# wo_B in the buffer of q's weights, M_B's units spread between two products: one change to a gated pair of linear-attention blocks

## The chip, the cores and the metric

The kernel runs on one core of a Trainium2 chip. The metric is device time in microseconds (us) for one execution. The profile is one execution of the same program, taken by the hardware profiler. The engines are called as the profile calls them: PE is TensorE (its weight loads are listed as PEld), DVE is VectorE, ACT is ScalarE, POOL is GpSimd, SP is SyncE. SP and ACT also issue DMAs; in the rows these stand as SPq and ACTq.

## What is computed

```python
def _A_ref(x, wqkv, wo):                      # _B_ref is the same with B's weights
    B, S, D = x.shape                         # 1, 2048, 640
    H = 32; Dh = D // H                       # 20
    q, k, v = ...                             # x @ wqkv, split, by heads
    phi = lambda t: jnp.where(t > 0, t + 1, jnp.exp(t)) + 1e-6
    pq, pk = phi(q), phi(k)
    kv = jnp.einsum("bhsd,bhse->bhde", pk, v)
    z = jnp.einsum("bhsd->bhd", pk)
    num = jnp.einsum("bhqd,bhde->bhqe", pq, kv)
    den = jnp.einsum("bhqd,bhd->bhq", pq, z)[..., None] + 1e-6
    return merge_heads(num / den) @ wo

x = A_x                                       # both blocks read A_x
g = sigmoid((x * gate_w).sum(-1, keepdims=True))
return g * _A_ref(x, A_wqkv, A_wo) + (1 - g) * _B_ref(x, B_wqkv, B_wo)
```

## The kernel before, in words

For each block b (A, then B) the kernel makes pk = phi(x Wk) by row chunks (`k_chunk`), pqT = phi(x Wq) transposed (`q_unit`), G = x^T pk (`g_all`, the row `gs` for its seven half-size products), the block-diagonal part of Wv^T G (`kv_mm` and `kv_mask`, tile KVA), and from that M = KVA wo, a 640x640 matrix (`m_a` for A, `m_b` for B). The gate and the denominators become rows R that scale pqT (`scale`). The output is pqT_A^T M_A + pqT_B^T M_B.

That last sum is a 2x2 block product: rows in two halves of 1024, columns in two halves of 320. It is done in seven products, P1 to P7, over eight pairs of row tiles (class `Pair`; pair i holds row tiles i and i+8). One product of one pair is five matmuls of 128x320 (`prod`, L586 to L592; in the profile all of them are line L590). P1 = pqT_A(lower rows) x M_A(left columns) and P5 = (pqT_A + pqT_B, upper rows) x TM[0], where TM[0] comes from M_A alone. P2, P3, P4, P6 and P7 need M_B, or differences TM[1..3] made from it. So P1 and P5 of the eight pairs, 16 x 5 matmuls, are what the kernel has to do while M_B is made.

M_B is made by six units, `m_b(0)` to `m_b(5)` (L784): two matmuls (L494, KVA rows times wo_B, one for each column half) into two PSUM banks, one copied by ACT and one by DVE (both L791) into a row of pk, then a store to DRAM (`m_store`, L500, queue of SP). After the six, `m_load(1)` (L503, SP) reads all of M_B back in the layout that the products need. The units use four single banks in turn, so unit k+2 writes the banks that unit k's copies empty.

P1 and P5 of one pair share a PSUM bank (`early`): P1 starts it, ACT copies it out (`p1_out`, L623), P5 adds onto it, ACT copies it out again (`p5_out`, L631). The bank then serves pair i+4. P5 of pair i reads upper rows i of pqT_A to which pqT_B has been added in place. That sum is `p_sums(..., (1,))` (L546): POOL makes it for pairs 0 and 1 (the first 256 rows), DVE makes it for pairs 2 and 3, 4 and 5, 6 and 7, in three instructions after the units' copies. DVE then makes the sums for P6 and P3 (also L546) and TM[1..3] (`m_sum`).

The order of everything here is written out by hand: the stages stand under `manual_schedule`, each engine takes its instructions in the order of the code, and the framework adds the semaphores. In the middle stage the order on PE is: P1 of pair 0; `kv_mm`; P1 of pairs 1 and 2; units 0, 1; P1 of pair 3; units 2, 3; P5 of pair 0; units 4, 5; then P5 of 1, P1 of 4 and 5, P5 of 2 and 3, P1 of 6 and 7, P5 of 4 to 7; then P2 (the rows `ow` and `oy`).

Weights go through the pool `wpool`, one buffer for each tag, and a tile of the same tag waits until the earlier one is no longer read. wo_B has the tag `wo`, which before it holds T13, operands of G's products for B. Its six DMAs (`load_wo`, L692 and L694, queue of SP) therefore stand in the code behind the last product that reads T13 (L424). R's second row for B is loaded by the queue of ACT (`r_load`, L543, called in L413).

At the end, the last pair does P7, then pair 6's P3, then its own P4, then its own P3 in two halves of 160 columns; each result is added by DVE (L595) and stored (L609).

Of the kernel before, what the change touches and what calls it, by code (L numbers as in the profile page):

```python
# [8 lines left out]
P = 128  # L9
FP32 = mybir.dt.float32  # L10
BF16 = mybir.dt.bfloat16
# [3 lines left out]
S, D, H = 2048, 640, 32  # L15
Dh = D // H
DT = D // P
# [4 lines left out]
HF = D // 2  # L22
TW = 4
WB = (120, 120, 80)
NW = 6
# [3 lines left out]
SH = S // 2  # L29
# [3 lines left out]
def kernel(  # L33
# [11 lines left out]
    nc = tc.nc  # L45
# [5 lines left out]
    wpool = ctx.enter_context(tc.tile_pool(name="wpool", bufs=1))  # L51
# [18 lines left out]
    xT = persist.tile([P, DT, S], BF16, name="xT")  # L70
    xn = persist.tile([P, ST, D], BF16, name="xn")
    pk = persist.tile([P, ST, D], BF16, name="pk")
    pqT = [persist.tile([P, DT, S], BF16, name=f"pqT{b}") for b in "AB"]
# [3 lines left out]
    M = [persist.tile([P, DT, D], BF16, name=f"M{b}") for b in "AB"]  # L77
    wo_sb = [None, None]
# [23 lines left out]
    TM = [early[:, 0:DT * HF].rearrange("p (c n) -> p c n", c=DT)] + [None] * 3  # L102
# [12 lines left out]
    wq = [None, None]  # L115
# [27 lines left out]
    for r in range(2):  # L143
        nc.gpsimd.memset(maskE[r][:], 1.0)
        for sign, base in ((1, 0), (-1, Dh - 1)):
            nc.gpsimd.affine_select(
                out=maskE[r][:], in_=maskE[r][:], pattern=[[-sign * Dh, WT[0] // Dh], [0, Dh]],
# [4 lines left out]
    for sign, base in ((1, 0), (-1, TW - 1)):  # L152
        nc.gpsimd.affine_select(
            out=headE[:], in_=headE[:], pattern=[[-sign * TW, H]],
# [220 lines left out]
    def g_strassen(b, den):  # L375

        x11, x12 = [xn[:, k:k + hc, 0:ic] for k in (0, hc)]
        x22 = xn[:, hc:ST, ic:2 * ic]
        b11 = pk[:, 0:hc, 0:HF]
        b21, b22 = [pk[:, hc:ST, n * HF:(n + 1) * HF] for n in range(2)]  # L380
        lo, hi = GT

        def temp(name):
            return work.tile([P, 2, HF], FP32, tag="osb", name=name, bufs=3)

        def add(dst, pt, sb):
            nc.vector.tensor_tensor(out=dst, in0=pt[:, :, 0:HF], in1=sb[:], op=ALU.add)

        even, odd = ps("gs0", 0), ps("gs1", 1)
        g_prod(even, x11, b11, True, 0, 1 - b)  # L390
        rec = den()
        rec(0)
        g_prod(even, x11, b11, True, 1 - b)
        p1 = temp("p1")
        nc.scalar.copy(out=p1[:], in_=even[:, :, 0:HF])
        if b == 0:
            x_sum(3)
        else:
            rec(1)
        g_prod(odd, SX[2], TK[b][2], True)  # L400
        u2 = temp("u2")
        add(u2[:], odd, p1)
        if b == 0:
            x_sum(4)
        else:
            p_diff(part[2])
            p_diff(part[3])
            m_sum(0)
        g_prod(even, x12, b21, False)
        nc.scalar.copy(out=lo[:, 0:2, :], in_=even[:, :, 0:HF])  # L410
        if b == 0:
            rec(1)
        r_load(b, 1, nc.scalar)  # L413
        if b == 0:
            wq[1] = load_w(1, "q", nc.scalar)
        scale(b, 0, 2, 0)
        g_prod(odd, SX[3], TK[b][3], False)
        u3 = temp("u3")
        add(u3[:], odd, p1)
        scale(b, 2, 4, 0)  # L420
        even = ps("gs0", 0)
        g_prod(even, SX[1], TK[b][1], True)
        if b == 1:
            load_wo(1, nc.sync)  # L424
        add(hi[:, 2:4, :], even, u3)
        scale(*((b, 0, 2, 1) if b else (b, 4, 5, 0)))
        g_prod(odd, x22, TK[b][4], False)
        if b == 1:
            scale(1, 4, 5, 0)
        add(lo[:, 2:4, :], odd, p1)  # L430
        if b == 1:
            scale(1, 2, 4, 1)
        g_prod(even, SX[4], b22, False)
        for n in range(2):
            nc.vector.tensor_tensor(out=hi[:, n, :], in0=even[:, n, 0:HF], in1=u2[:, n], op=ALU.add)
        if b == 0:
            scale(0, 0, 2, 1)
# [138 lines left out]
    def scale(b, lo, hi, h):  # L576

        dst = pqT[b][:, lo:hi, h * SH:(h + 1) * SH]
        nc.vector.tensor_tensor(
            out=dst, in0=dst, in1=R[h][:, None, :].to_broadcast([P, hi - lo, SH]), op=ALU.mult  # L580
        )
# [1 line left out]
    def rows_of(i):  # L583
        return out2[i * P:(i + 1) * P, :]

    def prod(dst, left, right, i, first):  # L586

        r0 = i * P
        for c in range(DT):
            nc.tensor.matmul(  # L590
                dst, lhsT=left[:, c, r0:r0 + P], rhs=right[:, c, :], start=(first and c == 0), stop=(c == DT - 1), skip_group_check=not first,
            )  # L592

    def out_add(dst, acc, sb):
        nc.vector.tensor_tensor(out=dst, in0=acc, in1=sb, op=ALU.add)  # L595
# [4 lines left out]
    class Pair:  # L600
# [4 lines left out]
            self.p1s, self.p15 = [xn[:, k * hc + i, :].bitcast(FP32) for k in range(2)]  # L605

        def store(self, k, lo=0, hi=D):
            eng = nc.scalar if self.last and (k or lo > HF) else nc.sync
            eng.dma_start(out=rows_of(self.i + k * (ST // 2))[:, lo:hi], in_=self.rows(k)[:, lo:hi])  # L609

        def at(self, bank):
# [2 lines left out]
        def early(self):  # L614
            return acc["xz"[self.i // 2 % 2]][self.i % 2][:, 0:HF]

        def p1(self, out=True):
            prod(self.early(), pqT[0][:, :, 0:SH], M[0][:, :, 0:HF], self.i, True)
            if out:
                self.p1_out()  # L620

        def p1_out(self):
            nc.scalar.copy(out=self.p1s, in_=self.early())  # L623

        def p5(self, out=True):
            prod(self.early(), pqT[0][:, :, SH:S], TM[0], self.i, False)
            if out:
                self.p5_out()

# [32 lines left out]
            out_add(self.rows(1)[:, 0:HF], self.at("x"), self.p1s)  # L662
            self.store(1, 0, HF if self.last else D)

        def p3(self):
            w = HF // 2
            parts = [(acc["z"][1 - n][:, 0:w], n * w, (n + 1) * w) for n in range(2)] if self.last else [(self.at("z"), 0, HF)]
            for dst, lo, hi in parts:
                prod(dst, xT[:, :, SH:S], M[1][:, :, HF + lo:HF + hi], self.i, True)
                out_add(self.rows(0)[:, HF + lo:HF + hi], dst, self.v[:, lo:hi])  # L670
                if self.last:
                    self.store(0, HF + lo, HF + hi)
            if not self.last:
                self.store(0)

    def load_w(b, which, eng, cuts=(0, DT)):
        lo = {"q": 0, "k": D, "v": 2 * D}[which]
        t = wpool.tile([P, DT, D], BF16, tag="w" + which, name=f"w{which}{'AB'[b]}")
        for c0, c1 in zip(cuts, cuts[1:]):
            eng.dma_start(out=t[:, c0:c1, :], in_=wq_dram[b][:, c0:c1, lo:lo + D])  # L680
        return t

    def load_wo(b, eng):
        t = wo_sb[b] = wpool.tile([P, NW, D], BF16, tag="wo", name=f"wo{'AB'[b]}")
        tv = t[:].rearrange("p (h i) f -> p h i f", h=2)
        wide = wo_dram[b].rearrange("(h r) f -> h r f", h=2)
        for r in range(2):
            p0 = r * P // 2
            for hf in range(2):
                src = wide[hf, 0:2 * WB[0], :].rearrange("(j p) f -> p j f", j=2)  # L690
                r0, n = r * WT[0], (P // 2, WT[0])[r]
                eng.dma_start(out=tv[p0:p0 + n, hf, 0:2, :], in_=src[r0:r0 + n])  # L692
            r0, n = 2 * WB[0] + r * WT[2], (P // 2, WT[2])[r]
            eng.dma_start(out=tv[p0:p0 + n, :, 2, :], in_=wide[:, r0:r0 + n, :].rearrange("h p f -> p h f"))  # L694
# [45 lines left out]
    with tc.manual_schedule():  # L740
# [34 lines left out]
        half = ST // 2  # L775
        acc = {k: [bank(outer, f"o{k}{n}") for n in range(2)] for k in "zx"}
        pairs = [Pair(i) for i in range(half)]
        with late_pool("mid") as mid:
            def single(k):
                return bank(mid, f"s{k}")  # L780

            first = [single(k) for k in range(4)]

            def m_b(k):  # L784
                part = pk[:, k, :].rearrange("p (b n) -> p b n", b=2)
                w = m_rows(k)[1]
                dst = [first[n] if k == 0 else single(k % 2 * 2 + n) for n in range(2)]
                for n in range(2):
                    m_mm(1, k, dst[n], n)
                for n, copy in enumerate((nc.scalar.copy, nc.vector.tensor_copy)):  # L790
                    copy(out=part[:w, n], in_=dst[n][:w, 0:HF])  # L791
                m_store(1, k, part)

            pairs[0].p1()
            scale(1, 4, 5, 1)
            kv = acc["z"][1]
            kv_mm(1, kv)
            kv_mask(kv)
            p_sums(slice(0, 2 * P), (1,), nc.gpsimd)
            pairs[1].p1()  # L800
            pairs[2].p1(False)
            m_b(0)
            m_b(1)
            pairs[2].p1_out()
            pairs[3].p1(False)
            m_b(2)
            m_b(3)
            pairs[0].p5(False)
            m_b(4)
            pairs[0].p5_out()  # L810
            m_b(5)
            m_load(1)
        pairs[1].p5()
        pairs[3].p1_out()
        for n in (1, 2, 3):
            p_sums(part[n], (1,))
        for k in range(2):
            pairs[4 + k].p1()
        for k in range(2):
            pairs[2 + k].p5()  # L820
        for k in range(2):
            pairs[6 + k].p1()
        for i in range(4, half):
            pairs[i].p5()
        for n in range(3):
            p_sums(part[n], (2, 4))
        inner = ctx.enter_context(late_pool("inner"))
# [13 lines left out]
        for i in range(half - 1):  # L841
            p, after = pairs[i:i + 2]
# [13 lines left out]
                p_sums(part[3], (later[i],))  # L856
        after.p7()
        p.p3()
        after.p4()
        after.p3()  # L860


# [28 lines left out]
```

## Time and profile before

| what | value |
|---|---|
| time, median of 3 runs | 182.66 us (182.41 to 183.09) |
| the profiled execution | 182.69 us |
| its span, first to last instruction | 180.9 us |
| granted TensorE clock | 1.000 |

The span leaves out 1.8 us of the profiled execution that lie around the program's instructions. A row of the timeline gives start, length, engine, line, operation, output<-inputs, the shape and the number of instructions that were merged, and in brackets the engine's idle time before them with what ended it. Lengths of pipelined matmuls overlap: the distance from one start to the next is what a matmul costs a busy PE.

### The profile page before, as it was taken

Reading aid. Unit: us, or ns where it says so; the run is one execution under the profiler, and the core shown is the slowest. Engines: PE = TensorE matmul, PEld = TensorE weight load, DVE = VectorE, ACT = ScalarE, POOL = GpSimd, SP = SyncE. Lnnn points to the kernel's source line nnn. Section 1 sums busy time; section 2 is a strip of 40 time slices with the busy share of each in tenths; the row PEclk is TensorE's granted clock in tenths of the full one; section 3 lists DMA queues with packets and bytes.
Section 4 is the critical chain, followed back from the end, with each engine's and each line's share of the span. In section 5 each row is a group of like instructions: output and inputs, shape, how many; then the busy total and the mean of one; then the engine's idle time right before and its main releaser. Section 6 shows DMA issues by size and latency. Waiting matters only on the chain.

```text
span 180.9 us, 3414 instructions
## 1 busy us (share of the span) xinstructions
PE 177.1 (98%) x1340; PEld 119.3 (66%) x1345; DVE 147.5 (81%) x247; ACT 85.8 (47%) x140; POOL 5.4 (3%) x18
## 2 busy tenths in 40 slices
PE   8999999999999999999999999999999999999993
PEld 4566657765577777777775555677777777677772
DVE  0386868989998896888778999969999799977863
ACT  2245846889971101378784779921101863111010
POOL 6000000000000000000000000000003200000000
PEclk9999999999999999999999999999999999999999
DMA  5999999523100216431116000000325451133323
GB/s 179 209 269 173 244 370 284 112 49 134 58 0 6 70 47 209 110 108 36 57 34 190 19 0 0 0 4 14 125 78 132 137 181 50 36 109 112 109 92 127
DMA packets 22842, 19.33 MB, mean 107 GB/s; under 512 B 10538, under 2 KB 22058, under 8 KB 22826
## 3 DMA queue, kind: packets, MB, share of 16 engines
q1 hardware_dynamic: 20744, 16.95, 34.0%
q10 hardware_dynamic: 2082, 2.17, 3.6%
q8 instruction: 10, 0.16, 0.4%
q14 instruction: 6, 0.05, 0.1%
HBM read 12.29 MB, written 4.53 MB: 93 GB/s over the span
## 4 chain that ended last, share of the span: by engine, by line
PE 97%; issue 0%; DVE 0%
PE gs L370 17%; PE kA L218 12%; PE ox L590 12%; PE kB L218 12%; PE qB L281 12%; PE qA L281 6%; PE oz L590 6%; PE qA L291 5%; PE gB L329 2%; PE gA L329 2%; PE ow L590 2%; PE xt L165 2%; PE qA L301 1%; PE mA L494 1%; PE s L494 1%; PE oy L590 1%
## 5 line engine op out<-in xcount | busy, mean ns | idle before, releaser
L218 PEld LDWEIGHTS <-xT 128*128 128x128 bf16 x320 | 31.0, 98 | 12.8 <-DVE xT L243 0.2
L210 DVE TENSOR_SCALAR e<-e 128x640 bf16<-128x640 bf16 (+2 forms) x53 | 18.9, 357 | 7.3 <-ACT e L205 6.7
L218 PE MATMUL kB<-wkB,xT 128*128 128x320 bf16 x160 | 23.1, 299 | 0.0
L218 PE MATMUL kA<-wkA,xT 128*128 128x320 bf16 (+1 forms) x160 | 22.9, 301 | 0.0
L281 PE MATMUL qB<-xT,wqB 128*128 128x512 bf16 x98 | 21.6, 379 | 0.1
L205 ACT ACTIVATE e<-kB 128x640 bf16<-128x640 f32 x16 | 11.2, 703 | 15.8 <-DMA wqB<-in_B_wqkv_dram 9.4
L281 PEld LDWEIGHTS <-wqB 128*128 128x128 bf16 x100 | 11.7, 117 | 9.7
L205 ACT ACTIVATE e<-kA 128x640 bf16<-128x640 f32 x16 | 11.2, 704 | 8.3 <-PE kA L218 8.3
L205 ACT ACTIVATE e<-qA 128x1024 bf16<-128x1024 f32 (+1 forms) x11 | 10.4, 946 | 6.4 <-PE qA L291 5.1
L648 ACT COPY u<-ox 128x320 f32<-128x320 f32 x8 | 3.4, 425 | 20.6 <-PE ox L590 20.6
L205 ACT ACTIVATE e<-qB 128x1024 bf16<-128x1024 f32 x10 | 10.2, 1023 | 5.6 <-PE qB L281 4.9
L370 PEld LDWEIGHTS <-xn 128*128 128x128 bf16 x96 | 9.2, 98 | 3.9 <-issue 0.4
L370 PEld LDWEIGHTS <-S 128*128 128x128 bf16 x96 | 9.4, 98 | 3.6
L281 PE MATMUL qA<-xT,wqA 128*128 128x512 bf16 x49 | 10.9, 379 | 0.1
L214 DVE SCALAR_TENSOR_TENSOR pk<-kB,e 128x640 bf16<-128x640 f32 x12 | 9.9, 824 | 1.2
L590 PEld LDWEIGHTS <-xT 128*128 128x128 bf16 x85 | 8.1, 98 | 2.9
L590 PEld LDWEIGHTS <-pqTB 128*128 128x128 bf16 x80 | 7.8, 98 | 3.3 <-issue 0.2
L590 PEld LDWEIGHTS <-pqTA 128*128 128x128 bf16 x80 | 7.7, 98 | 2.9
L370 PE MATMUL gs<-pk,xn 128*128 128x320 bf16 x64 | 9.5, 299 | 0.0
L281 PEld LDWEIGHTS <-wqA 128*128 128x128 bf16 x50 | 5.9, 117 | 4.8
L291 PE MATMUL qA<-xT,wqA 128*128 128x512 bf16 x38 | 8.9, 379 | 0.1
L212 DVE TENSOR_TENSOR pk<-pk,e 128x640 bf16<-128x640 bf16 x12 | 5.9, 492 | 2.8 <-ACT pk L209 2.2
(123 smaller groups left out, 296.9 us busy)
## 6 DMA issues: line engine op xcount, KB each, us to landing
xn<-in_A_x_dram SPq DMA_DIRECT2D x1, 2240.0 KB, 10.0
out_dram<-pk SPq DMA_DIRECT2D x14, 160.0 KB, 1.8
wvA<-in_A_wqkv_dram SPq DMA_DIRECT2D x1, 800.0 KB
wkB<-in_B_wqkv_dram SPq DMA_DIRECT2D x1, 800.0 KB, 4.7
wqB<-in_B_wqkv_dram ACTq DMA_DIRECT2D x1, 800.0 KB, 6.5
wvB<-in_B_wqkv_dram SPq DMA_DIRECT2D x1, 800.0 KB
MA<-mA_dram SPq DMA_DIRECT2D x1, 800.0 KB, 6.1
MB<-mB_dram SPq DMA_DIRECT2D x1, 800.0 KB
```

The lines of the kernel that those rows point to most:

```text
L165: nc.tensor.matmul(warm[:, 1, 0:n], lhsT=one_l, rhs=one_r[:, 0:n], start=True, stop=True)
L205: nc.scalar.activation(out=e[:], in_=src, func=ACT.Exp)
L210: nc.vector.tensor_scalar(e[:], e[:], 1.0, EPS, op0=ALU.min, op1=ALU.add)
L212: nc.vector.tensor_tensor(out=dst, in0=dst, in1=e[:], op=ALU.max)
L214: nc.vector.scalar_tensor_tensor(out=dst, in0=src, scalar=1.0 + EPS, in1=e[:], op0=ALU.add, op1=ALU.max)
L218: nc.tensor.matmul(pt[:, hf, 0:w], lhsT=xT[:, c, i * P:(i + 1) * P], rhs=wk[b][:, c, hf * HF:hf * HF + w], start=(c == 0), stop=(c == DT - 1),
L281: nc.tensor.matmul(pt[:, u, :], lhsT=mixed(wq[b][:, c, :], m), rhs=xT[:, c, n * HB:(n + 1) * HB], start=(c == 0), stop=(c == DT - 1),)
L291: nc.tensor.matmul(pt[:, u, :], lhsT=mixed(wq[b][:, c, :], m + u), rhs=xT[:, c, n * HB:(n + 1) * HB], start=(c == 0), stop=(c == DT - 1),)
L329: nc.tensor.matmul(pt[:, hf, 0:HF], lhsT=xn[:, i, c * P:(c + 1) * P], rhs=pk[:, i, hf * HF:(hf + 1) * HF], start=(i == 0), stop=(i == ST - 1),
L370: nc.tensor.matmul(pt[:, n, 0:HF], lhsT=left[:, i, n * P:(n + 1) * P], rhs=right[:, i, :], start=(first and i == 0), stop=(i == hc - 1), s ...
L494: nc.tensor.matmul(dst[:w, 0:HF], lhsT=KVA[:rows, k, 0:w], rhs=wo_sb[b][:rows, k, n * HF:(n + 1) * HF], start=True, stop=True,)
L590: nc.tensor.matmul(dst, lhsT=left[:, c, r0:r0 + P], rhs=right[:, c, :], start=(first and c == 0), stop=(c == DT - 1), skip_group_check=not ...
```

## The change

- wo_B takes the tag `wq`: its buffer is that of q's weights for B, which are last read by `q_unit`. Its six DMAs are issued by ACT instead of SP, right behind R's second row, and stand in the code before the products that used to free its buffer.
- The units of M_B: two matmuls of P1 (pair 2) ahead of unit 0, two ahead of unit 1, then one, two, one, two matmuls of P1 (pair 2) and P5 (pair 0) ahead of units 2 to 5. Before, whole products of five matmuls stood between pairs of units. P1 of pair 3 leaves this stretch.
- `p1_out` of pair 2 and `p5_out` of pair 0 come behind all six units on ACT.
- The rest of P1 and P5 has a new order: P1 of 3; P5 of 1, 2; P1 of 4; P5 of 3; P1 of 5, 6; P5 of 4; P1 of 7; P5 of 5, 6, 7.
- At the end, the last pair's P4 stands between the two halves of its P3. The store of the first half goes to the queue of ACT and that of the second to SP's; before it was the other way round.

```diff
@@ g_strassen
         if b == 0:
             wq[1] = load_w(1, "q", nc.scalar)
+        else:
+            load_wo(1, nc.scalar)
...
         g_prod(even, SX[1], TK[b][1], True)
-        if b == 1:
-            load_wo(1, nc.sync)
@@ prod, Pair.p1 and Pair.p5 take the matmuls' numbers
-        for c in range(DT):
+        for c in cs:
@@ Pair.store
-            eng = nc.scalar if self.last and (k or lo > HF) else nc.sync
+            eng = nc.scalar if self.last and (k or lo == HF) else nc.sync
@@ Pair.p3
+        def p3(self, n=None):
+            lo, hi = (0, HF) if n is None else (n * HF // 2, (n + 1) * HF // 2)
+            dst = acc["z"][(self.i + (n or 0)) % 2][:, 0:hi - lo]
+            prod(dst, xT[:, :, SH:S], M[1][:, :, HF + lo:HF + hi], self.i, True)
+            out_add(self.rows(0)[:, HF + lo:HF + hi], dst, self.v[:, lo:hi])
+            self.store(0, 0 if n is None else HF + lo, HF + hi)
@@ load_wo
-        t = wo_sb[b] = wpool.tile([P, NW, D], BF16, tag="wo", name=f"wo{'AB'[b]}")
+        t = wo_sb[b] = wpool.tile([P, NW, D], BF16, tag=("wo", "wq")[b], name=f"wo{'AB'[b]}")
@@ the middle stage
             pairs[1].p1()
-            pairs[2].p1(False)
-            m_b(0)
-            m_b(1)
-            pairs[2].p1_out()
-            pairs[3].p1(False)
-            m_b(2)
-            m_b(3)
-            pairs[0].p5(False)
-            m_b(4)
-            pairs[0].p5_out()
-            m_b(5)
+            fill = [(step, c) for step in (pairs[2].p1, pairs[0].p5) for c in range(DT)]
+            for k, n in enumerate((2, 2, 1, 2, 1, 2)):
+                for step, c in fill[:n]:
+                    step(False, (c,))
+                fill = fill[n:]
+                m_b(k)
             m_load(1)
-        pairs[1].p5()
-        pairs[3].p1_out()
+        pairs[2].p1_out()
+        pairs[0].p5_out()
         for n in (1, 2, 3):
             p_sums(part[n], (1,))
-        for k in range(2):
-            pairs[4 + k].p1()
-        for k in range(2):
-            pairs[2 + k].p5()
-        for k in range(2):
-            pairs[6 + k].p1()
-        for i in range(4, half):
-            pairs[i].p5()
+        p1s, p5s = [[(step, i) for i in range(half)] for step in (Pair.p1, Pair.p5)]
+        for step, i in (*p1s[3:4], *p5s[1:3], p1s[4], p5s[3], *p1s[5:7], p5s[4], p1s[7], *p5s[5:]):
+            step(pairs[i])
@@ the end
         p.p3()
+        after.p3(0)
         after.p4()
-        after.p3()
+        after.p3(1)
```

More of the change, by code (lines that the diff above doesn't have):

```diff
@@ L584, in rows_of, with prod @@
         return out2[i * P:(i + 1) * P, :]
-    def prod(dst, left, right, i, first):
+    def prod(dst, left, right, i, first, cs=range(DT)):
         r0 = i * P
-        for c in range(DT):
+        for c in cs:
             nc.tensor.matmul(
@@ L615, in early, with p1 @@
             return acc["xz"[self.i // 2 % 2]][self.i % 2][:, 0:HF]
-        def p1(self, out=True):
-            prod(self.early(), pqT[0][:, :, 0:SH], M[0][:, :, 0:HF], self.i, True)
+        def p1(self, out=True, cs=range(DT)):
+            prod(self.early(), pqT[0][:, :, 0:SH], M[0][:, :, 0:HF], self.i, True, cs)
             if out:
@@ L623, in p1_out, with p5 @@
             nc.scalar.copy(out=self.p1s, in_=self.early())
-        def p5(self, out=True):
-            prod(self.early(), pqT[0][:, :, SH:S], TM[0], self.i, False)
+        def p5(self, out=True, cs=range(DT)):
+            prod(self.early(), pqT[0][:, :, SH:S], TM[0], self.i, False, cs)
             if out:
@@ L663, in p4 @@
             self.store(1, 0, HF if self.last else D)
[L665 to L674, printed above, removed]
+        def p3(self, n=None):
[4 more added lines that the diff above has]
+            self.store(0, 0 if n is None else HF + lo, HF + hi)
     def load_w(b, which, eng, cuts=(0, DT)):
```

## The prediction

> **What bounds the kernel now.** I read the page first: busy shares, then the chain of work that ended last.
>
> ```profile
> span 180.9 us, 3414 instructions
> ...
> PE 177.1 (98%) x1340; PEld 119.3 (66%) x1345; DVE 147.5 (81%) x247; ACT 85.8 (47%) x140; POOL 5.4 (3%) x18
> ...
> PE 97%; issue 0%; DVE 0%
> ```
>
> PE is busy in 98% of the span and carries 97% of the chain. The list of waits, for PE alone, has one row:
>
> ```profile
> PE xt L165 <- PEq L875: 0.8, 1, 0.8
> ```
>
> That is the start of the program. So no engine and no DMA holds PE up by more than fractions of a us. The stretches around the change say the same (columns: stretch; its length; busy us and count of PE, PEld, DVE, ACT, POOL; clock; DMA share; GB/s):
>
> ```profile
> 139.42:143.11 3.69, 3.69 (x30) 2.99 (x27) 2.58 (x8) 2.47 (x7) 2.03 (x1) 1.00 0.27 82
> 143.11:150.58 7.47, 7.47 (x57) 5.38 (x55) 7.34 (x11) 5.36 (x14) 0.00 (x0) 1.00 0.57 182
> 148.00:150.00 2.00, 2.00 (x17) 1.47 (x15) 1.97 (x3) 1.28 (x3) 0.00 (x0) 1.00 0.86 347
> 150.00:150.25 0.25, 0.25 (x4) 0.17 (x3) 0.22 (x2) 0.15 (x1) 0.00 (x0) 1.00 0.02 0
> ```
>
> The first is the stretch of M_B's units, the second is the rest of P1 and P5 while M_B goes to DRAM and back. PE is full in both at clock 1.00. The last two show how near M_B is: DMAs run until about 150.0, and the first matmul that reads M_B starts at 150.58, with no gap ahead of it.
>
> The change neither removes nor adds a matmul (the last P3 was in halves already). On a full PE it can only win what PE still waits for, and lose where the new order brings a matmul ahead of its operand. I therefore work out, for each moved step, when PE would reach it and when its operand is there.
>
> **M_B's units.** PE, from the second product behind the kv matmuls:
>
> ```profile
> 139.43 0.84 PE L590 MATMUL oz<-MA,pqTA 128*128 128x320 bf16 x5
> 140.11 0.71 PE L494 MATMUL s<-woB,KVA 124*120 124x320 bf16 x4
> 140.65 0.84 PE L590 MATMUL oz<-MA,pqTA 128*128 128x320 bf16 x5
> 141.33 0.71 PE L494 MATMUL s<-woB,KVA 104*80 104x320 bf16 x4
> 141.88 0.84 PE L590 MATMUL ox<-TM,pqTA 128*128 128x320 bf16 x5
> 142.56 0.71 PE L494 MATMUL s<-woB,KVA 124*120 124x320 bf16 x4
> ```
>
> Five matmuls take 140.11 - 139.43 = 0.68, so one takes 0.136, in the units too (0.54 for four). Before, 27 matmuls fill 139.43 to 143.11. What else runs there (POOL first, then DVE; the PE row is the start of the kv matmuls):
>
> ```profile
> 138.84 2.61 POOL L546 TENSOR_TENSOR pqTA<-pqTA,pqTB 128x1280 bf16<-128x1280 bf16 x1 [135.37 <-PE oz L462]
> 137.20 0.89 DVE L435 TENSOR_TENSOR GT<-gs,u 128x320 bf16<-128x320 f32 x2
> 137.77 0.40 PE L462 MATMUL oz<-GT,wvB 128*60 128x60 bf16 x14
> 138.85 0.82 DVE L475 TENSOR_TENSOR KVA<-oz,maskE 60x240 bf16<-60x240 f32 x2 [0.16 <-PE oz L462]
> 140.58 0.89 DVE L791 CAST pk<-s 120x320 bf16<-120x320 f32 x2 [0.39 <-PE s L494]
> 143.03 0.89 DVE L791 CAST pk<-s 120x320 bf16<-120x320 f32 x2 [0.34 <-PE s L494]
> 143.95 2.29 DVE L546 TENSOR_TENSOR pqTA<-pqTA,pqTB 128x1280 bf16<-128x1280 bf16 x3
> ```
>
> The POOL row is the key. It adds pqT_B to the 256 rows that P5 of pairs 0 and 1 read, and ends at 138.84 + 2.61 = 141.45. Before, P5 of pair 0 starts at 141.88, so its 0.43 of slack hides that sum. Nothing that starts POOL moves.
>
> After the change PE does, from 139.43: two matmuls of P1, unit 0, two, unit 1, one, unit 2, and then the first matmul of P5 of pair 0. That is 5 + 6 = 11 matmuls, 1.50, so P5 is due at 140.93. First a small term: unit 0 would start at 139.43 + 2 x 0.136 = 139.70, and the masks it reads end at 138.85 + 0.82 = 139.67. The kv matmuls started at 137.77 on an operand whose first half DVE finished at about 137.69 (the first of the two in the DVE row at 137.20, about 0.49 long), so a released load costs some 0.07: unit 0 starts at 139.75, **0.05 late**, and P5 is due at 140.98. It can start at 141.45 + 0.07 = 141.52, **0.54 late**. PE takes its matmuls in order, so units 3, 4 and 5 wait behind it.
>
> The banks cost nothing: unit k+2 comes five matmuls (0.68) after unit k, and a copy ends about 0.34 + 0.49 = 0.83 after its matmul starts (0.34 from the start of a unit's second matmul, 140.11 + 0.136 = 140.25, to DVE at 140.58; half of the row's pair is about 0.49). From the start of that matmul to the same bank's next use there are 7 slots, 0.95. That holds while DVE is free, and its four masks end about 140.2, just as unit 0's copy is due.
>
> From 141.52 there are 11 matmuls left in this stretch: it ends at 143.02 instead of 143.11, but with 22 matmuls done instead of 27. In PE's work that is 0.59 late.
>
> **P1 and P5 in the new order.** P1 of pair 3 and P5 of pair 1 follow, to 143.02 + 1.36 = 144.38. Then comes P5 of pair 2, which before stood two products later. It reads the first of DVE's three sums (0.82 each). DVE makes that behind the copy of unit 5, which ends about 0.82 after that unit's last matmul starts (142.88): at 143.70. Before, the sum began 0.03 after the copy's end (143.92 to 143.95), so it runs from 143.73 to 144.56, and with 0.07 P5 starts at 144.63, **0.25 late**. All later steps find their sums and banks ready: DVE's next two sums end 0.74 apart, and each bank has at least two products (1.36) between a product and the next use, against about 0.34 + 0.43 for a copy by ACT, also with the two copies that now stand behind the units.
>
> Sum of the middle: 0.05 + 0.54 + 0.25 = **+0.84**. P2 starts at about 151.42 instead of 150.58.
>
> **wo_B and M_B.** Loads of the same kind, and what surrounds them:
>
> ```profile
> 132.84 1.31 SPq L692 DMA_DIRECT2D woB<-in_B_wo_dram  x2
> 129.06 0.55 ACTq L543 DMA_DIRECT2D R<-rB_dram  x1
> 137.88 0.43 ACT L623 COPY xn<-ox 128x320 f32<-128x320 f32 x1 [8.64 <-PE ox L590]
> 133.59 1.22 DVE L579 TENSOR_TENSOR pqTB<-pqTB,R 128x2048 bf16<-128x2048 bf16 x1
> R<-rA_dram ACTq DMA_DIRECT2D x1, 256.0 KB, 3.0
> wqB<-in_B_wqkv_dram ACTq DMA_DIRECT2D x1, 800.0 KB, 6.5
> 141.13 3.22 SPq L500 DMA_DIRECT2D mB_dram<-pk  x6
> 146.23 0.35 SPq L503 DMA_DIRECT2D MB<-mB_dram  x1
> ```
>
> The first issue moves from 132.84 to about 129.61, behind R's row on ACT. Six issues at the SP row's 0.65 take 3.9, to 133.5; ACT has no other work until 137.88, so they delay nothing. Could they delay R? In block A the same row on the same queue has q's weights (800 KB) right behind it and lands 3.0 after its issue; so R lands by about 132.1, and DVE first needs it at 133.59. wo_B, at the 6.5 of that larger load, is there by 136.1, far ahead of 139.70. Cost 0, gain 0: PE did not wait for wo_B before. M_B's last store is 0.2 earlier (143.70 against 143.92), so M_B lands near 149.9, 1.5 ahead of the new P2. That slack is what the change buys, and in this execution nobody waited for it.
>
> **What comes back, and the end.** DVE's sums and P2's additions make PE wait once in the output stage:
>
> ```profile
> 155.33 0.84 PE L590 MATMUL ox<-TM,xT 128*128 128x320 bf16 x5
> 155.65 0.48 DVE L595 TENSOR_TENSOR pk<-ox,xn 128x320 bf16<-128x320 f32 x1
> 156.19 0.43 PE L590 MATMUL ox<-TM,pqTB 128*128 128x320 bf16 x2
> ```
>
> From 155.33 to 156.19 there are 0.86 for five matmuls: 0.17 lost, released by the DVE row that ends at 156.13. DVE's backlog there starts with its sums, which come 0.2 earlier, while PE comes 0.84 later. The wait goes: **-0.17**.
>
> ```profile
> 176.66 0.84 PE L590 MATMUL ox<-TM,pqTB 128*128 128x320 bf16 x5
> 177.34 0.85 PE L590 MATMUL oz<-MB,xT 128*128 128x160 bf16 x10
> 177.54 0.49 DVE L595 TENSOR_TENSOR pk<-ox,xn 128x320 bf16<-128x320 f32 x1 [0.25 <-PE ox L590]
> 177.94 0.61 DVE L595 TENSOR_TENSOR pk<-oz,v 128x160 bf16<-128x160 f32 x2
> ```
>
> At the end, P4 waited some 0.06 for the addition of P7; half a P3 (five of 0.069) now covers that. But P4's addition moves next to the last one: P4's last matmul is now 0.29 later, DVE adds it from 177.83 to 178.32 and the last half until 178.55, where it also ends now. **0.**
>
> Sum: +0.84 - 0.17 = +0.67 on a span of 180.9 and a time of 182.69: 183.36. The median shown is 0.03 lower, so I forecast **183.35 us**, 0.4% slower.
>
> **Rivals.**
>
> *POOL's sum takes longer* (the slower side). The POOL row is seen beside two of DVE's copies; in the new order a third one, 0.49, falls into it. If POOL stands still while DVE copies, it ends 0.49 later, every bit of it before P5 of pair 0: 183.84. It decides from the first 0.01 on, since the slack is gone. Against it: the row gives no sign that POOL was stopped before.
>
> *POOL doesn't hold PE*. If the two copies beside it (0.89) were part of its 2.61, it could be as short as 1.72 and end at 140.56, before 140.98. That leaves 0.05 + 0.25 - 0.17 = +0.13: 182.8. It would need the copies to stay out of it, and they don't: they come earlier.
>
> The Trainium skill ("SBUF — State Buffer", Who interferes with whom) states that a DVE instruction with at most one SBUF input, outside its 2-port modes, doesn't contend with GpSimd. The copies and the masks read PSUM, so by that rule POOL's 2.61 stays, neither of these two happens, and the sum is the one above; no run here shows POOL without DVE beside it.
>
> *M_B was late in ordinary runs.* It lands within 0.6 of its use. If executions without the profiler wait x for it, the change gives x back: 183.35 - x. For faster by 0.5%, x would have to be 1.6. Against it: the profiled execution shows no wait and took 182.69, the median is 182.66 and the fastest 182.41.
>
> *It doesn't do what it says*: should the first P5 matmul and DVE's sum be released as early as PE comes, only -0.17 is left, 182.5.
>
> **Chances.** About 0.5% (0.9 us) is what a measurement of this kernel can tell from no change. Forecast (183.1 to 183.75) 0.57, of which 0.17 above 183.57; POOL longer, or another stall of that size that I missed in so tight an order, 0.22; POOL not in the way 0.1; no stall at all 0.05; M_B late 0.06. That makes slower 0.39, same 0.55, faster 0.06. The range leaves out M_B's case and the rest of the longer stalls: 182.5 to 184.1.
>
> **What would show it.** In the profile after: a gap on PE of about 0.5 ahead of the first `ox<-TM,pqTA` matmul, which starts when the POOL row ends, near 141.5; one of about 0.25 ahead of P5 of pair 2 near 144.6; the first `ow` near 151.4, with DMAs quiet since about 150; no gap at the first `ox<-TM,pqTB`; wo_B's DMAs under ACTq from 129.6. I am wrong if POOL's sum ends before 141, if DVE's first sum is there before 144.4, or if the span shrinks with PE gaps as forecast, for then something before 139 moved.

## The result and the profile after

The changed kernel takes 183.24 us (median of 7 executions, 183.11 to 184.04) against 182.66; the ratio is 1.0044 with a 95% interval of 1.0025 to 1.0064. The profiled execution took 183.24 with a span of 181.5. From the page:

```profile
span 181.5 us, 3423 instructions
...
PE 177.0 (98%) x1345; PEld 118.5 (65%) x1345; DVE 147.7 (81%) x247; ACT 86.2 (47%) x140; POOL 5.4 (3%) x18
```

PE does the same work (it has 1345 weight loads in both, so five records of matmuls are missing among the 1340 before) and the span is 0.6 longer. The list of waits, asked for PE's weight loads, now names what was on no list before:

```profile
PEld L590 <- POOL pqTA L546: 0.6, 1, 0.6
...
PEld L590 <- DVE pqTA L546: 0.4, 1, 0.4
...
PEld L494 <- DVE KVA L475: 0.2, 1, 0.2
```

A weight load normally runs ahead of PE, so these times are longer than what PE loses. What PE loses is read from the starts in its timeline:

```profile
139.33 0.43 PE L590 MATMUL oz<-MA,pqTA 128*128 128x320 bf16 x2
139.62 0.48 PE L494 MATMUL s<-woB,KVA 124*120 124x320 bf16 x2
...
140.63 0.43 PE L494 MATMUL s<-woB,KVA 104*80 104x320 bf16 x2
141.40 0.45 PE L590 MATMUL ox<-TM,pqTA 128*128 128x320 bf16 x2 [0.33 <-POOL pqTA L546]
...
142.92 0.84 PE L590 MATMUL oz<-MA,pqTA 128*128 128x320 bf16 x5
143.60 0.84 PE L590 MATMUL ox<-TM,pqTA 128*128 128x320 bf16 x5
144.52 0.85 PE L590 MATMUL oz<-TM,pqTA 128*128 128x320 bf16 x5
```

Unit 2 starts at 140.63 and has two matmuls, 0.27; the first P5 matmul starts at 141.40 instead of 140.90. From 143.60 five matmuls reach to 144.28; P5 of pair 2 starts at 144.52. What they waited for, POOL's row and then DVE's (the copies of the six units, and behind them the three sums):

```profile
138.74 2.60 POOL L546 TENSOR_TENSOR pqTA<-pqTA,pqTB 128x1280 bf16<-128x1280 bf16 x1 [135.25 <-PE oz L462]
```

```profile
140.15 1.45 DVE L787 CAST pk<-s 120x320 bf16<-120x320 f32 x3
142.16 1.45 DVE L787 CAST pk<-s 120x320 bf16<-120x320 f32 x3 [0.57 <-PE s L494]
143.63 2.29 DVE L546 TENSOR_TENSOR pqTA<-pqTA,pqTB 128x1280 bf16<-128x1280 bf16 x3
```

POOL ends at 141.34, and DVE's first sum (0.82 of this row) at about 144.45: both matmuls start 0.06 to 0.07 later. The first matmul that reads M_B, and the one that waited for DVE in the output stage:

```profile
151.32 1.52 PE L590 MATMUL ow<-MB,pqTB 128*128 128x320 bf16 x10
...
156.07 0.84 PE L590 MATMUL ox<-TM,xT 128*128 128x320 bf16 x5
156.75 0.43 PE L590 MATMUL ox<-TM,pqTB 128*128 128x320 bf16 x2
```

Counted from the first matmul behind the kv matmuls (138.64 here, 138.74 before; both rows stand below), P2 starts after 12.68 instead of 11.84: 0.84 later, the forecast's sum for the middle. From 156.07 to 156.75 there are 0.68 for five matmuls: the wait of 0.17 before is gone. In stretches of M_B's load (columns as in the prediction), DMAs now go quiet by 149.5, 1.8 ahead of P2:

```profile
147.00:149.50 2.50, 2.50 (x20) 1.82 (x19) 2.47 (x4) 1.49 (x5) 0.00 (x0) 1.00 0.75 300
149.50:149.75 0.25, 0.25 (x4) 0.17 (x3) 0.25 (x1) 0.25 (x1) 0.00 (x0) 1.00 0.01 0
```

The end, PE and then DVE:

```profile
177.51 0.84 PE L590 MATMUL ox<-TM,pqTB 128*128 128x320 bf16 x5
178.19 0.51 PE L590 MATMUL oz<-MB,xT 128*128 128x160 bf16 x5
```

```profile
178.39 0.49 DVE L595 TENSOR_TENSOR pk<-ox,xn 128x320 bf16<-128x320 f32 x1 [0.30 <-PE ox L590]
178.79 0.31 DVE L595 TENSOR_TENSOR pk<-oz,v 128x160 bf16<-128x160 f32 x1
```

P4 takes its 0.68 with no gap, and DVE's last addition ends at 179.10. Counted as above that is 40.46, against 39.81 before: 0.65 later, so what is lost is lost ahead of the end.

**A common start for comparing executions.** The kernels are equal up to the kv matmuls (but for wo_B's issue), and still the first matmul behind them starts between 138.30 and 139.07 in the profiles of this study (e9 and e10 apart, which are told below). That difference is there by the first matmul of q: it starts at 10.48 in the earliest of them (e11) and at 11.25 in the latest (e12). It comes from the start of the program, where PE waits for x and the first weights for varying times. So I compare each profile by what is left after that start ("rest": span less start; the page gives the span to 0.1, so it is good to some 0.05). Before:

```profile
138.74 0.85 PE L590 MATMUL ox<-MA,pqTA 128*128 128x320 bf16 x5
```

and after:

```profile
138.64 0.85 PE L590 MATMUL ox<-MA,pqTA 128*128 128x320 bf16 x5
```

The rest is 180.9 - 138.74 = 42.16 before and 181.5 - 138.64 = 42.86 after: **0.70 longer**, where the timed medians differ by 0.58 and the ratio of 1.0044 stands for 0.80.

### The profile page after: what moved, and what is told of

Same layout as the page of the kernel before. It is cut to its first block, busy times and chain, and to the rows that moved or that the text cites. A ratio compares the mean times of both kernels' runs of the same rounds, so it can differ in the third digit from the quotient of the medians.

```text
span 181.5 us, 3423 instructions
## 1 busy us (share of the span) xinstructions
PE 177.0 (98%) x1345; PEld 118.5 (65%) x1345; DVE 147.7 (81%) x247; ACT 86.2 (47%) x140; POOL 5.4 (3%) x18
## 4 chain that ended last, share of the span: by engine, by line
PE 89%; DVE 4%; DMA 3%; POOLq 1%; ACTq 1%; issue 0%; DVEq 0%
PE gs L370 14%; PE kB L218 12%; PE qB L281 12%; PE kA L218 11%; PE ox L590 11%; PE qA L281 6%; PE oz L590 5%; PE qA L291 5%; DMA wkA<-in_A_wqkv_dram 3%; PE gA L329 2%; PE gB L329 2%; PE ow L590 2%; DVE pqTB L579 2%; POOLq L873 1%; PE qA L301 1%; PE mA L494 1%
```

## The experiments

The theory: PE waits about 0.5 for POOL's sum and 0.24 for DVE's first sum, because P5 of pairs 0 and 2 come earlier than their operands; the rest of the change is worth nothing, or gives 0.17 back. Rivals 1 to 4 stand in the expectations. All ratios are to the kernel before, timed beside the run on the same chip, where its medians were 182.68 (e1 to e4), 182.74 (e5 to e8), 182.78 (e9 to e11) and 182.79 (e12); a ratio need not be that of the medians.

| run | median us (executions) | ratio, 95% interval | start | rest |
|---|---|---|---|---|
| before | 182.66 (7) | | 138.74 | 42.16 |
| changed | 183.24 (7) | 1.0044 (1.0025 to 1.0064) | 138.64 | 42.86 |
| e1: P1 as filling, old order | 182.66 (12) | 1.0009 (0.9994 to 1.0023) | 138.79 | 42.11 |
| e2: P1 as filling, new order | 183.01 (11) | 1.0018 (1.0007 to 1.0029) | 138.64 | 42.36 |
| e3: P5 of pair 2 later | 183.16 (9) | 1.0029 (1.0018 to 1.0040) | 138.49 | 42.61 |
| e4: POOL sums 384 rows | 184.38 (4) | 1.0091 (1.0078 to 1.0104) | 138.77 | 43.83 |
| e5: wo_B's move alone | 182.72 (11) | 1.0001 (0.9990 to 1.0012) | 138.65 | 42.95 |
| e6: the new end alone | 182.62 (12) | 0.9994 (0.9984 to 1.0003) | 138.53 | 42.17 |
| e7: changed, old end | 183.53 (6) | 1.0051 (1.0037 to 1.0064) | 138.80 | 42.90 |
| e8: e1 with the old end | 182.80 (12) | 1.0023 (0.9999 to 1.0047) | 138.53 | 42.17 |
| e9: wo_B's move alone, on SP | 183.51 (6) | 1.0043 (1.0029 to 1.0057) | 139.54 | 42.16 |
| e10: e8 with wo_B on SP | 183.74 (6) | 1.0067 (1.0042 to 1.0092) | 139.55 | 42.15 |
| e11: changed, again | 183.81 (6) | 1.0046 (1.0029 to 1.0064) | 138.30 | 42.90 |
| e12: changed, wo_B not moved | 183.64 (6) | 1.0047 (1.0029 to 1.0065) | 139.07 | 42.93 |

Each start and rest is read from one profiled execution. By the timed intervals alone, e1 and e4 are told from the changed kernel, but e2 and e3 are not: the steps between e1, e2, e3 and the changed kernel rest on their profiles, and the ratios stand in the same order.

**e1, both waits taken away.** P1 of pair 3 needs nothing from POOL.

```diff
-            fill = [(step, c) for step in (pairs[2].p1, pairs[0].p5) for c in range(DT)]
+            fill = [(step, c) for step in (pairs[2].p1, pairs[3].p1) for c in range(DT)]
...
         pairs[2].p1_out()
-        pairs[0].p5_out()
+        pairs[0].p5()
+        pairs[3].p1_out()
...
-        for step, i in (*p1s[3:4], *p5s[1:3], p1s[4], p5s[3], *p1s[5:7], p5s[4], p1s[7], *p5s[5:]):
+        for step, i in (p5s[1], *p1s[4:6], *p5s[2:4], *p1s[6:8], *p5s[4:]):
```

> The changed kernel with one part replaced: between M_B's units stand the matmuls of P1 of pairs 2 and 3 (P5 of pair 0 comes behind the units), and behind them the order of the kernel before. wo_B's move, the unit spacing and the end stay as changed. Theory (PE waits 0.49 for POOL's sum and 0.24 for DVE's first sum): both gaps vanish, the gap of 0.17 ahead of the first P4 stays away, so 182.4 to 182.6, slightly below the kernel before. Rival 1 (the close spacing of the units costs, by banks and copies): stays at 183.1 to 183.2. Rival 2 (wo_B's load beside R on ACT's queue costs): also stays at 183.2.

The list of waits for weight loads, from 130 to 178, has lost both sums and kept the mask:

```profile
PEld L462 <- issue: 0.3, 1, 0.3
PEld L494 <- DVE KVA L475: 0.2, 1, 0.2
```

The rest is 42.11, below the changed kernel by 0.75 and below the kernel before by 0.05. The units stand as close as in the changed kernel, and wo_B and the end are moved: rivals 1 and 2 fall as causes of the 0.70. The median of 182.66 is 0.06 above the expected range, and the ratio's interval holds 1. The 12 executions lie in two parts, 7 from 182.34 to 182.68 and 5 from 183.15 to 183.45.

**e2, the wait for POOL alone taken away.** As e1, with the changed kernel's order behind the units.

```diff
+        for step, i in (*p5s[1:3], p1s[4], p5s[3], *p1s[5:7], p5s[4], p1s[7], *p5s[5:]):
```

> As the run before, but behind the units the changed kernel's order with P5 of pair 0 in the place of P1 of pair 3, so P5 of pair 2 is the third product behind the units. It removes the wait for POOL alone. Theory: the gap of 0.49 goes, the one of about 0.25 ahead of P5 of pair 2 stays: 182.7 to 182.8. Rival 3 (DVE's first sum only looks late because PE was held up by POOL before it): no gap, 182.5. Rivals 1 and 2: 183.2.

```profile
PEld L590 <- DVE pqTA L546: 0.4, 1, 0.4
PEld L462 <- issue: 0.3, 1, 0.3
PEld L494 <- DVE KVA L475: 0.2, 1, 0.2
```

DVE's sum is still waited for, POOL's not; the rest falls by 0.50. Rival 3 falls: DVE's sum is late by itself. The median of 183.01 lies above the expected 182.7 to 182.8; the profiled execution took 182.75.

**e3, the wait for DVE's sum alone taken away.**

```diff
-        for step, i in (*p1s[3:4], *p5s[1:3], p1s[4], p5s[3], *p1s[5:7], ...):
+        for step, i in (p1s[3], p5s[1], p1s[4], *p5s[2:4], *p1s[5:7], ...):
```

> The changed kernel with P5 of pair 2 one product later (P1 of 3, P5 of 1, P1 of 4, then P5 of 2). It removes the wait for DVE's first sum alone. Theory: the gap of 0.49 at POOL's sum stays, the one of 0.24 goes: 183.0. Rival 3: 183.2, with the gap moved elsewhere, or not there to remove.

```profile
141.25 0.44 PE L590 MATMUL ox<-TM,pqTA 128*128 128x320 bf16 x2 [0.33 <-POOL pqTA L546]
...
143.44 0.84 PE L590 MATMUL ox<-TM,pqTA 128*128 128x320 bf16 x5
144.12 0.84 PE L590 MATMUL ox<-MA,pqTA 128*128 128x320 bf16 x5
144.80 1.39 PE L590 MATMUL oz<-TM,pqTA 128*128 128x320 bf16 x9
```

The wait for POOL stays, and P5 of pair 2 (144.80) follows at PE's pace. The rest falls by 0.25, as the gap says. The median of 183.16 is off the expected 183.0; its profiled execution took 182.84.

**e4, POOL's sum made longer.**

```diff
-            p_sums(slice(0, 2 * P), (1,), nc.gpsimd)
+            p_sums(slice(0, 3 * P), (1,), nc.gpsimd)
...
-        for n in (1, 2, 3):
-            p_sums(part[n], (1,))
+        for rows in (slice(3 * P, 4 * P), part[2], part[3]):
+            p_sums(rows, (1,))
```

> The changed kernel with POOL's sum over 384 rows instead of 256 (it also makes pair 2's), DVE's first sum over 128 rows less. Theory (POOL's end sets PE's time one to one): POOL takes 2.60 x 1.5 = 3.9 and ends 1.3 later, PE's gap there grows from 0.49 to 1.8, the gap at P5 of pair 2 (0.24) goes: 184.2 to 184.4. Rival 1 or 2: POOL is not what PE waits for, and the time stays within 0.2 of 183.2.

POOL's row, and PE's:

```profile
138.87 3.81 POOL L546 TENSOR_TENSOR pqTA<-pqTA,pqTB 128x1920 bf16<-128x1920 bf16 x1 [135.40 <-PE oz L462]
```

```profile
140.77 0.44 PE L494 MATMUL s<-woB,KVA 104*80 104x320 bf16 x2
142.75 0.45 PE L590 MATMUL ox<-TM,pqTA 128*128 128x320 bf16 x2 [1.54 <-POOL pqTA L546]
```

POOL takes 1.21 more, PE's gap is 142.75 - 141.04 = 1.71 (1.22 more), the gap at P5 of pair 2 goes, and the rest is 0.97 longer than the changed kernel's: 1.21 - 0.24. POOL's end sets the time one to one.

**e5, wo_B's move alone**, on the kernel before: the diff's first two parts and the buffer's tag.

> The kernel before with wo_B's move alone (q's buffer, ACT's queue behind R's row). Theory: PE waited for wo_B nowhere, R is there in time: 182.6 to 182.7, runs spread as before. Rival 4, new: the runs so far with wo_B's move and the new end fall into two groups 0.7 apart (182.3 to 182.7 and 183.1 to 183.5 in the first experiment), the kernel before doesn't. If wo_B's early load makes that second group (R late in some executions), it is seen here, and not in the next run.

The median is the one expected. But its profiled execution took 183.34, and shows a wait that no other profile has:

```profile
149.54 1.11 PE L590 MATMUL oz<-TM,pqTA 128*128 128x320 bf16 x7
151.41 1.38 PE L590 MATMUL ow<-MB,pqTB 128*128 128x320 bf16 x9 [0.76 <-DMA MB<-mB_dram]
```

P2 is due at 150.49 and starts at 151.41: 0.92 lost to M_B. In stretches:

```profile
148.00:150.00 2.00, 2.00 (x17) 1.43 (x16) 1.97 (x3) 1.25 (x3) 0.00 (x0) 1.00 0.74 288
150.00:150.25 0.25, 0.25 (x4) 0.17 (x3) 0.22 (x2) 0.24 (x1) 0.00 (x0) 1.00 0.06 26
150.25:151.25 1.00, 0.40 (x3) 0.16 (x2) 0.69 (x1) 0.61 (x2) 0.00 (x0) 1.00 0.05 19
```

The load is over at 150, as in the kernel before, but for a share of 0.05 to 0.06 of 16 DMA engines, about one of them, which goes on for another us.

**e6, the new end alone**, on the kernel before: `p3`, the store's queue and the last four calls as in the diff.

> The kernel before with the new end alone (the last P4 between P3's halves, the halves' stores on swapped queues). Theory: 0, or 0.07 slower, since PE ends 0.06 earlier and DVE's last addition does not: 182.6 to 182.8. Rival 4 turned round: if the new end makes the second group (the last store on SP's queue), the runs fall into two groups 0.7 apart here and not in the run before.

0, as expected: the rest is 42.17 against 42.16, no execution is above 182.88. **e7**, the changed kernel with the old end, agrees with a rest of 42.90 against 42.86:

> The changed kernel with the end of the kernel before. Theory: as the changed kernel, 183.1 to 183.2. If the second group comes from the new end, there is one group near 183.1; if from wo_B's move, both groups stay.

e7's median of 183.53 lies above the expected 183.1 to 183.2, with executions from 183.35 to 183.95; the profiled one took 183.40. **e8** has e1's order and the old end:

> The first experiment (P1 of pairs 2 and 3 between the units, the order of before behind them, wo_B's move) with the end of the kernel before: no gap at POOL's sum, at DVE's first sum or ahead of the first P4. Theory: 182.4 to 182.5, a little under the kernel before. If the second group comes from the new end, one group near 182.45; if from wo_B's move, two groups, median 182.5 to 183.

Its rest is that of the kernel before (42.17), its profiled execution took 182.40, but its median is 182.80, with four executions of 12 from 183.49 to 185.06. So the new end is not what makes the upper parts.

**e9 and e10, wo_B issued by SP**, in e5 and e8:

```diff
-            load_wo(1, nc.scalar)
+            load_wo(1, nc.sync)
```

> The kernel before with wo_B in the buffer of q's weights, but issued by SP (where nothing holds it any more, so behind R's first row). The kernel with wo_B on ACT's queue had a median equal to the kernel before, but 2 of 11 executions at 183.3, and the one that was profiled waits 0.76 for M_B, one part of which lands late. Theory A (in that execution a fetch of instructions of 16 KB ran into M_B's load; a matter of chance that has nothing to do with the queue of wo_B): a few executions near 183.3 here too, median 182.6 to 182.8. Theory B (wo_B's six issues on ACT bring it about): no execution above 183.2, median 182.6. Rival: R's first row, needed as soon as it lands, is delayed by wo_B right behind it: 182.8 to 183.5 in all executions, with DVE waiting for R near 129.7.

> The eighth experiment (P1 of pairs 2 and 3 between the units, order and end of before) with wo_B issued by SP. All gaps removed that were found, M_B's load about 0.9 earlier than in the kernel before. Theory A: best executions at 182.4, some at 183.3 and above, median 182.5 to 182.8. Theory B: one group, 182.3 to 182.6, faster than the kernel before by 0.1 to 0.2. Rival as in the run before: 182.8 to 183.5.

The rival of these two won. DVE's timeline and PE's in e9:

```profile
130.35 1.23 DVE L579 TENSOR_TENSOR pqTB<-pqTB,R 128x2048 bf16<-128x2048 bf16 x1 [0.78 <-DMA R<-rB_dram]
```

```profile
137.74 0.71 PE L462 MATMUL oz<-GT,wvB 128*60 128x60 bf16 x36
138.73 0.22 PE L462 MATMUL oz<-GT,wvB 128*60 128x60 bf16 x2 [0.28 <-DVE GT L435]
139.13 0.49 PE L462 MATMUL oz<-GT,wvB 128*60 128x60 bf16 x22 [0.18 <-DVE GT L435]
```

In e9 R's first row is 0.7 late for DVE with wo_B behind it on the same queue, and R's second row holds DVE up for another 0.41 (in e10 the two waits are 0.51 and 0.65). DVE's whole chain shifts, and the kv matmuls wait for it: both runs come to the stage that the change is about some 0.8 late (139.54 and 139.55 against 138.74). From there on they lose nothing (rest 42.16 and 42.15). So it matters when wo_B's loads are issued: from 127.22 on by SP, behind R's first row, or from 129.64 on by ACT, behind its second (the changed kernel). Queue, place and time change together here; which of them counts is not separated.

**e11 and e12, the changed kernel again, and without wo_B's move** (old tag, SP, old place).

> The changed kernel once more, beside these. Theory: 183.1 to 183.3 for most executions, the same gaps (0.49 at POOL's sum, 0.24 at DVE's first sum). The first seven executions reached from 183.11 to 184.04; if M_B's landing late by chance makes the upper ones, about a third of these lie above 183.6 too.

> The changed kernel without wo_B's move (its old buffer, SP, its old place in the code); units, order and end as changed. The executions of the changed kernel reach from 182.9 to 184.0, with a part near 183.2 and a part near 183.8, and those of the kernel before only from 182.3 to 183.2. Theory B (wo_B's six loads right behind R's second row hold R up in some executions, as they do in every execution when SP issues them behind R's first row): all executions near 183.2 to 183.4, none above 183.6; wo_B lands at about 139.7, as unit 0 comes, so a gap of up to 0.1 there may be new. Theory A (M_B's load lands late by chance): the two parts stay. Both: the gap at POOL's sum stays 0.4 to 0.5, that at DVE's first sum 0.24.

e11's gaps are those of the first profile, and so is the rest. But most executions were expected at 183.1 to 183.3, and five of the six lie from 183.62 to 183.92, one, the profiled, at 182.88. e12's rest is the same within 0.1 (no gap at unit 0 beyond the changed kernel's), and its executions go from 183.36 to 183.90. So theory B falls: the upper part is there without wo_B's move. Theory A is not shown either, since only one profile, e5's, holds a late M_B. What the profiles do show is the start: 138.30 in e11's profiled execution, which took 182.88, and 139.07 in e12's, which took 183.68. They are 0.77 apart at the start and 0.80 in time, with the same rest, so between these two the start makes nearly all of the difference.

No version was shown to beat both kernels: the intervals of e1, e6 and e8 all hold 1.

## Why the prediction was right

The forecast was 183.35 (0.67 more on the profiled execution); measured were 183.24 and 0.70 on the rest. The mechanism is the forecast one. That the median came within 0.11 is in part luck: the same kernel's second set of executions (e11, beside 182.78 for the kernel before) has a median of 183.81. By its steps:

- **PE is the bound, and the change moves no work.** Right: PE is at 98% in both, and every experiment's rest follows from its gaps alone.
- **Unit 0 waits for the masks, 0.05.** From 139.33 two matmuls reach to 139.60; unit 0 starts at 139.62, and the next two matmuls at 139.94 instead of 139.89. So 0.07, of which 0.05 stand behind unit 0's first matmul, whose weight load had waited for the masks (the row of L494 in the list above).
- **P5 of pair 0 waits for POOL, 0.54.** 0.50 by the timeline, 0.50 by e2, and by e4 one to one. Of the 0.04 that the term is too large, 0.02 went to the masks' wait; POOL and the release were 0.01 shorter each.
- **P5 of pair 2 waits for DVE's sum, 0.25.** 0.24 by the timeline, 0.25 by e3. The three gaps make 0.81 of the 0.84 that P2 is late; the other 0.03 are in no single gap.
- **The wait in the output stage goes, -0.17.** It went.
- **wo_B's move and the end: 0.** e5 and e6 have ratios of 1.0001 and 0.9994, e7 and e12 the changed kernel's rest.
- **M_B earlier is a slack that nobody waits for.** Right in the profiles of the kernel before and the changed kernel. M_B came earlier than forecast: DMAs are quiet by 149.5, where it was to land near 149.9. But e5, which has the order of before, shows that M_B can land 0.9 too late for P2, so the rival "M_B was late" has a real mechanism. Whether the kernel before has such executions is not shown. If it has, they are few: its 84 executions in all sets lie between 182.26 and 183.37, with medians from 182.66 to 182.79.
- **The rival of a longer POOL sum** did not come: 2.61 with two copies of DVE beside it, 2.60 with two and the first half of a third (DVE's row from 140.15 on). That agrees with the rule of the Trainium skill ("SBUF — State Buffer", Who interferes with whom) that instructions of DVE with at most one SBUF input, outside its 2-port modes, don't contend with GpSimd.

What the forecast did not hold is the spread. The changed kernel's 13 executions lie between 182.88 and 184.04; that is 1.16 wide, where the 84 of the kernel before are 1.11 wide. The start of the program accounts for up to 0.77 between profiles, and it accounts for the time of e12's profiled execution (183.68). Whether it, M_B or something else puts most executions of e11 near 183.8 stays open, as no profile of that kernel fell there.

## What to carry to other kernels

When the bound engine has no gaps, a new order of the same work can hardly win, and it loses wherever a moved step's operand is not ready when the engine now comes to it. So write down, for every step that moves forward, who makes its operand and when that ends. The slow helper (here one instruction on POOL, 2.6 long) is the first to look at, because its row shows no wait as long as a later consumer hides it. Filling with steps that need only old operands (P1 instead of P5 in e1) gave back all of the loss in the profile (rest 42.11 against 42.16 before).

To compare changes of a few tenths of a us, compare profiles from a common instruction on, not spans: the start here varied more than the effect.

## What was not expected of the hardware

- Loads under way at the same time delayed each other by more than this change is worth, and not on one queue alone. In e9, with wo_B's loads right behind R's first row (256 KB) on SP's queue, DVE waits 0.78 for that row; in the kernel before DVE's multiplication followed 0.07 behind the instruction ahead of it (129.66 after 129.59). R's second row had nothing queued behind it on ACT's queue in e9, and it landed 5.5 after its issue at 129.09 (5.4 in e10). In the kernel before it was issued at 129.06, and the DMA share is 0.00 from 132.00 to 134.00, so it had landed within 3.0. Nor does a load behind it on its own queue slow a row each time: in block A the row on ACT's queue with 800 KB behind it had landed in 3.0. The Trainium skill ("DMA: Bandwidth & Descriptors", Queues, rings and completion order) says that descriptors are consumed in ring order and promises no order of completion. What makes the rows slower was not taken apart.
- M_B's load of 800 KB ended one us late in one execution (e5), with a DMA share of 0.05 to 0.06, as of one of 16 DMA engines, after the others were done in time. What held it up stays open.
